# Rows as sixteen quarter-array products, index products in bf16, and a new table of places, in a fused attention and expert kernel

## The chip, the cores and the metric

The kernel runs on one core of one Trainium2 chip. The metric is the device time of one execution in microseconds (us); the kernel before has a median of 632.37 us over three runs (632.0 to 633.66).

## The reference, cut to what matters

Attention over 8 batches, 8 heads, 576 positions and 64 values per head, causal with a window of 128 and a linear bias per head; its output is the input of a layer of 8 experts, of which each token takes the one with the highest gate.

```python
scores = scale * np.matmul(q, k.transpose(0, 1, 3, 2))
scores = np.where((rel >= 0) & (rel < 128), scores + bias[None], -1e9)
attn = exp(scores - max); attn = attn / (sum + 1e-09)
x = np.matmul(attn, v).transpose(0, 2, 1, 3).reshape(B * S, H * D)     # 4608 x 512
logits = x @ w_gate                                                    # 8 experts
expert_idx = np.argmax(logits, axis=1); gate_w = softmax(logits)[expert_idx]
out[token] = gate_w[token] * (relu(x[token] @ w1[e]) @ w2[e])          # e = expert_idx[token]
```

## The kernel before

**Attention** goes over 36 chunks of 128 queries. Each chunk passes through named steps, each a few instructions on one engine:

- S00, S01, S10, S11 (`scores`, lines 201 and 206): TensorE puts bias and scores of two head pairs each into `s_ps`; there are two such buffers (g = 0, 1), one deep.
- N0, N1 (`peak`): VectorE folds and takes the negated maximum. E0, E1 (`exps`, line 228): ScalarE takes the exponentials, four instructions with an accumulator read each.
- T (`transposes`, line 242): sixteen products on TensorE into `t_ps`. P (`place`, line 250): ScalarE copies them to `pT`; GpSimd masks the window's ends (lines 253, 256).
- V, U, W, Z (`values`, line 283): products with v into `r_ps`, for one chunk or a pair. X (`copy_x`): a copy of `r_ps` to `xT`, on ScalarE for the chunks in `X_ACT` (line 293), on VectorE for the others (line 295).
- R (`rows`, line 304): `xT` times `iw`, which holds the gate's columns beside an identity, so that rows of x and the parts of the logits come out together, 72 columns a product; they go to `t_ps`, or to `s_ps` for the chunks in `ASIDE`. I, Y (`invert`, `scale_rows`, line 318): VectorE divides by the sums, and a DMA writes the rows to `xd` in device memory.

**Routing** follows in groups of three to six chunks (`route`, a generator that is resumed piece by piece): maxima, one-hot, ranks within an expert, and last the index products (line 650), which add into `base` which token stands in which slot of which expert. Their left side `lp` (128x128 per chunk, line 617) and right side `rr` (128x48, line 646) come from VectorE.

**The experts** come after: for each, gathers of its tokens' rows, two layers of which each is three products of rounded and rest parts (lines 828 and 1033), and a scatter of the result. The first layer of the largest expert's first 256 tokens is done within the end of attention (`EP`), and the weights are rounded by ScalarE and GpSimd throughout (lines 1145 and 1150).

What sets the order: up to step 147 every engine's instructions go out in the order in which the program is written. A chunk has four steps of time; the tables `PLACES`, `ALONE`, `FIRST`, `SECOND`, `BEFORE_ALONE`, `END`, `ROUND`, `REST`, `EP` and `PACE` give for each piece the step relative to its chunk and a rank within the step. Loads go out on SyncE at set steps, each made to wait for the last product before it. `WU` is the number of products of zeros (line 157) at the start and in steps 0 to 3.

```python
for k, (at, rank) in places(ch).items():
    plan.setdefault(4 * ch + at, []).append((rank, ch, k))
```

Of the kernel before, what the change touches and what calls it, by code (L numbers as in the profile page):

```python
# [425 lines left out]
ALONE = {'V': (14, 0.9), 'U': (15, 3), 'X': (16, 0.5)}
FIRST = {'X': (19, 5.5)}
SECOND = {'V': (11, 2.5), 'U': (11, 3), 'W': (14, 0.9), 'Z': (14, 2.2), 'X': (17, 0.3)}
BEFORE_ALONE = {'V': (11, 0.7), 'U': (11, 1.5), 'W': (12, 4.5), 'Z': (12, 5.5), 'X': (17, 0.3)}
QAT = (11, 0.5)  # L430
PIECES = ((1, 20),)
# [60 lines left out]
LB = 1
LW = (0, 0, 0, 0)
WU = (6, 3, 0, 0, 0)
APART_TO = 27
# [937 lines left out]
```

## Time and profile before

| | |
|---|---|
| median of three runs | 632.37 us (632.0 to 633.66) |
| profiled execution | 635.56 us, span 633.5 us |
| granted TensorE clock, mean | 0.992 |
| TensorE busy | 609.1 us (96%) |
| VectorE, ScalarE, GpSimd busy | 371.9, 298.2, 313.8 us (59%, 47%, 50%) |
| bytes moved | 99.17 MB, mean 157 GB/s |

The span is the time from the first to the last instruction of the profiled execution; the time of an execution is some 2 us longer. PE is TensorE's products, PEld its weight loads, which overlap them; DVE is VectorE, ACT ScalarE, POOL GpSimd. A product of fp32 operands stands in the trace as two records, one of bf16 operands as one. A product's duration includes its way through the array, so that several overlap: what a piece takes of TensorE's time is read from its start to the start of the next piece.

### The profile page before, as it was taken

The page shows a single profiled execution, that of the slowest core. Times are in us where ns is not written, and L with a number is a line of the kernel's source. Part 1 is how long each engine was busy: PE and PEld are TensorE (multiplying, and loading weights), DVE is VectorE, ACT ScalarE, POOL GpSimd, SP SyncE. Part 2 cuts the span into 40 slices and gives each one's busy share as a digit, 9 for nine tenths or more (in the row PEclk, how much of TensorE's full clock was granted, in tenths as well). Part 3 has the DMA queues.
Part 4 walks back from the last instruction along what each step waited for, and adds up shares of the span by engine and source line. Part 5 has one row for each costly group of instructions (what it writes and reads, how often), then busy time and mean ns, then how long its engine had stood idle before and what let it go on. Part 6 is the DMA issues. An engine that isn't in the chain of part 4 may idle for free.

```text
span 633.5 us, 17303 instructions
## 1 busy us (share of the span) xinstructions
PE 609.1 (96%) x6833; PEld 527.1 (83%) x6833; DVE 371.9 (59%) x875; ACT 298.2 (47%) x897; POOL 313.8 (50%) x465
## 2 busy tenths in 40 slices
PE   7989998999999989999999999999999999999996
PEld 5777887887878868888988898998898998888884
DVE  5667878778767775535543754555355356347411
ACT  6988887788654225423342434334233333424311
POOL 5766976877853031265236607633660760561202
PEclk9999999999979999999999999999999999999999
DMA  8777787677453265372544325434443542544201
GB/s 283 248 223 242 228 257 221 210 255 247 132 168 98 87 198 162 111 270 75 215 124 145 110 88 180 118 112 133 143 119 95 174 140 74 187 113 150 68 1 62
DMA packets 46902, 99.17 MB, mean 157 GB/s; under 512 B 12053, under 2 KB 13077, under 8 KB 46818
## 3 DMA queue, kind: packets, MB, share of 16 engines
q1 hardware_dynamic: 38194, 76.82, 37.9%
q0 software_dynamic: 8336, 20.96, 11.3%
q8 instruction: 55, 0.90, 0.6%
q10 hardware_dynamic: 288, 0.26, 0.2%
q14 instruction: 29, 0.24, 0.1%
HBM read 77.93 MB, written 20.09 MB: 155 GB/s over the span
## 4 chain that ended last, share of the span: by engine, by line
PE 76%; issue 9%; ACT 6%; POOL 4%; DVE 3%; DMA 1%; POOLq 0%; ACTq 0%; DVEq 0%
PE y_ps L1033 26%; PE l_ps L828 26%; PE r_ps L283 5%; PE s_ps L206 4%; PE t_ps L304 4%; ACT pe L228 3%; ACT pT L250 2%; PE t_ps L242 2%; PE s_ps L201 2%; PE s_ps L828 2%; PE s_ps L650 1%; POOL out L1021 1%; DVE nmax L218 1%; POOL pT L253 1%; POOL pT L256 1%
## 5 line engine op out<-in xcount | busy, mean ns | idle before, releaser
L835 DVE SCALAR_TENSOR_TENSOR hl<-l_ps,hh 128x320 fp32r<-128x320 f32 (+4 forms) x104 | 51.8, 502 | 153.4 <-ACT hh L831 127.7
L831 ACT ACTIVATE hh<-l_ps 128x320 fp32r<-128x320 f32 (+4 forms) x104 | 46.0, 447 | 202.1 <-PE l_ps L828 158.3
L808 POOL DMA_INDIRECT xg<-xd,od_idx x112 | 115.1, 1028 | 35.1 <-issue 33.1
L228 ACT ACTIVATE pe<-s_ps,nmax 128x128 f32<-128x128 f32 x288 | 102.1, 379 | 19.9 <-DVE nmax L218 11.8
L1033 PE MATMUL y_ps<-wh,hh 128*128 128x512 f32 x280 | 110.0, 393 | 0.1
L1033 PE MATMUL y_ps<-wl,hh 128*128 128x512 f32 x280 | 109.3, 390 | 0.0
L1033 PE MATMUL y_ps<-wh,hl 128*128 128x512 f32 x280 | 109.1, 390 | 0.0
L1021 POOL DMA_INDIRECT out<-y,od_pidx x33 | 34.4, 1043 | 144.8 <-ACT y L1039 138.6
L1133 DVE TENSOR_TENSOR wl<-w_raw,wh 128x512 fp32r<-128x512 f32 x114 | 73.9, 689 | 27.7 <-ACT wh L1129 21.0
L828 PE MATMUL l_ps<-xh,wh 128*128 128x320 f32 (+8 forms) x416 | 81.2, 317 | 0.2 <-ACT xh L787 0.2
L828 PE MATMUL l_ps<-xl,wh 128*128 128x320 f32 (+8 forms) x416 | 80.7, 315 | 0.7 <-issue 0.7
L828 PE MATMUL l_ps<-xh,wl 128*128 128x320 f32 (+8 forms) x416 | 80.4, 315 | 0.7 <-issue 0.7
L828 PEld LDWEIGHTS l_ps<-xh,wh 128*128 128x128 f32 x416 | 67.7, 188 | 7.4 <-issue 1.2
L828 PEld LDWEIGHTS l_ps<-xl,wh 128*128 128x128 f32 x416 | 65.9, 188 | 3.6 <-issue 1.6
L828 PEld LDWEIGHTS l_ps<-xh,wl 128*128 128x128 f32 x416 | 65.8, 188 | 2.2 <-issue 0.3
L228 ACT ACTIVATION_READ_ACCUMULATOR pe<-s_ps,nmax 128x1 f32 x288 | 62.6, 217 | 0.0
L1033 PEld LDWEIGHTS y_ps<-wh,hl 128*128 128x128 f32 x280 | 52.6, 188 | 11.4
L1033 PEld LDWEIGHTS y_ps<-wh,hh 128*128 128x128 f32 x280 | 52.6, 188 | 10.2 <-issue 0.6
L1129 ACT CAST wh<-w_raw 128x1024 fp32r<-128x1024 f32 x57 | 59.5, 1044 | 1.6 <-DMA w_raw<-w 1.4
L1033 PEld LDWEIGHTS y_ps<-wl,hh 128*128 128x128 f32 x280 | 52.6, 188 | 9.2
L206 PE MATMUL s_ps<-k_sb,q_sb 64*64 64x192 f32 (+2 forms) x1152 | 59.0, 314 | 0.0
L253 POOL TENSOR_SCALAR_AFFINE_SELECT pT<-pT 64x512 f32<-64x512 f32 x56 | 37.5, 670 | 34.6 <-ACT pT L250 32.5
(237 smaller groups left out, 905.9 us busy)
## 6 DMA issues: line engine op xcount, KB each, us to landing
w_raw<-w SPq DMA_DIRECT2D x56, 512.0 KB
v_sb<-v SPq DMA_DIRECT2D x36, 256.0 KB
xd<-x_sb SPq DMA_DIRECT2D x32, 288.0 KB
q_sb<-qT SPq DMA_DIRECT2D x35, 256.0 KB
k_sb<-kT SPq DMA_DIRECT2D x23, 256.0 KB
w_raw<-w SPq DMA_DIRECT2D x16, 256.0 KB
w_n<-w SPq DMA_DIRECT2D x4, 1024.0 KB
k_sb<-kT SPq DMA_DIRECT2D x8, 384.0 KB
```

The lines of the kernel that those rows point to most:

```text
L206: anchor(nc.tensor.matmul(out=heads[half(a), c, n, 64 * u0:].rearrange("q (u x) -> q u x", x=64), lhsT=blocks["q", ch][half(c), 2 * g + n, ...
L228: nc.scalar.activation(out=pes[ch][:, 2 * g + n, :, c, :], in_=s_ps[g][:, c, 192 * n + 64:192 * n + 192].rearrange("q (u x) -> q u x", x=6 ...
L253: nc.gpsimd.affine_select(out=to[half(c), :, 0], in_=to[half(c), :, 2], pattern=[[0, 8], [-1, 64]], base=-1, channel_multiplier=1, compare ...
L283: anchor(nc.tensor.matmul(out=tops[half(p % 2), c, p // 2, i:i + n, :], lhsT=blocks["v", j][half(c), r, p, :], rhs=diagonal(pTs[group], ha ...
L808: ins = tc.nc.gpsimd.indirect_dma_start(out=g[:, s], out_offset=None, in_=parts, in_offset=bass.IndirectOffsetOnAxis(ap=idx[:, s], axis=0),)
L828: nc.tensor.matmul(out=ps, lhsT=a[:, 128 * d:128 * d + 128], rhs=b[:, d], start=(k == 0), stop=(k == 11))
L831: nc.scalar.activation(out=hh, in_=ps, func=AF.Relu)
L835: nc.vector.scalar_tensor_tensor(out=hl, in0=ps, scalar=0.0, in1=hh.bitcast(F32), op0=ALU.max, op1=ALU.subtract)
L1021: ins = nc.gpsimd.indirect_dma_start(**kw).ins
L1033: nc.tensor.matmul(out=ys[t], lhsT=a[:, tl], rhs=b[:, 512:1024], start=(f == 0 and k == 0), stop=(f == 7 and k == 2))
L1129: keep(tc, nc.scalar.copy(out=wh, in_=raw))
L1133: keep(tc, eng.tensor_tensor(out=wl[:, sl], in0=raw[:, sl], in1=wh.bitcast(F32)[:, sl], op=ALU.subtract))
```

## The change

- `rows`: each 64x128 product is split into two of 64x64, one per half of the queries; 16 products a chunk in place of 8. With two halves of the contraction and two of the output, four tiles of the array are used in turn.
- Routing: `lp` is bf16 with two buffers in place of fp32 with one; the token's number is split into two bf16 parts (`tokh`, `tokl`), so `rr` has two parts and there are two bf16 products per chunk in place of one in fp32. The constant `tok` goes.
- `X_ACT` names 17 chunks in place of 6.
- `WU` goes from (6, 3, 0, 0, 0) to (7, 4, 1, 2, 2).
- The tables of attention's places are new, most of them by a step or a rank; `ROUND`, `REST` and the entries of chunks 0 and 1 stay. `END`, which overrides the general places for single chunks, has entries for 30 chunks in place of 11. Two or three entries of `EP` and `PACE` move by a step.
- A pad of 160 bytes (`EPAD`) in one pool.

```diff
     def rows(ch):
         for p in range(0, NP, 2):
             for c in range(2):
-                for e in range(2):
-                    anchor(nc.tensor.matmul(out=row_bank(ch)[:, e, HW * (p + c):HW * (p + c) + HW],
-                                            lhsT=xT[half(e), c, p // 2].rearrange("d a q -> d (a q)"),
-                                            rhs=iw_sb[half(e), p // 2, c, :], start=True, stop=True))
+                for a in range(2):
+                    for e in range(2):
+                        anchor(nc.tensor.matmul(out=row_bank(ch)[half(a), e, HW * (p + c):HW * (p + c) + HW], lhsT=xT[half(e), c, p // 2, a, :],
+                                                rhs=iw_sb[half(e), p // 2, c, :], start=True, stop=True))
...
-PLACES = {'S10': (-1, 9), 'S11': (0, 2), 'E0': (0, 2.5), 'T': (5, 0.7), 'N1': (1, 0.7), 'P': (5, 0.95), 'S00': (-3, 4.7), 'S01': (-3, 6), 'R': (22, 1), 'E1': (2, 2), 'N0': (-2, 1.5), 'I': (21, 0.5), 'Y': (23, 1.8)}
+PLACES = {'S10': (-1, 9), 'S11': (0, 2), 'E0': (0, 0.95), 'T': (5, 0.7), 'N1': (1, 1.8), 'P': (5, 6.5), 'S00': (-3, 3.7), 'S01': (-3, 6.5), 'R': (22, 1), 'E1': (2, 2), 'N0': (-2, 2.5), 'I': (21, 9), 'Y': (23, 2.5)}
...
-X_ACT = (20, 21, 25, 32, 33, 34)
+X_ACT = (3, 7, 9, 10, 11, 12, 13, 14, 15, 16, 20, 21, 25, 26, 32, 33, 34)
...
-LB = 1
-WU = (6, 3, 0, 0, 0)
+WU = (7, 4, 1, 2, 2)
...
-    lp = rp.tile(sp3, F32, name="lp", bufs=LB)
+    lp = rp.tile(sp3, BF16, name="lp")
...
-    rr = rp.tile(sc3, F32, name="rr")
-    nc.vector.tensor_tensor(out=rr, in0=eq, in1=st["tok"][:, c0:c0 + G].unsqueeze(2).to_broadcast(sc3), op=ALU.mult)
+    rr = rp.tile([128, G, 2, E * TT], BF16, name="rr")
+    for k, n in enumerate(("tokh", "tokl")):
+        nc.vector.tensor_tensor(out=rr[:, :, k, :], in0=eq,
+                                in1=st[n][:, c0:c0 + G].unsqueeze(2).to_broadcast(sc3), op=ALU.mult)
     yield
     ip = spare(st, 1, E * TT)
     for g in range(G):
-        nc.tensor.matmul(out=ip, lhsT=lp[:, g, :], rhs=rr[:, g, :], start=g == 0, stop=g == G - 1)
+        for k in range(2):
+            nc.tensor.matmul(out=ip, lhsT=lp[:, g, :], rhs=rr[:, g, k, :], start=(g == k == 0),
+                             stop=(g == G - 1 and k == 1))
```

Three places in the order of instructions, each from before and from the change.

TensorE, the first group's index products and the next rows, before (`lp`, `rr` are the sides of the index products, `pT` and `v_sb` those of the values):

```order
L206 MATMUL s_ps<-k_sb,q_sb 64x192 x8
L650 MATMUL s_ps<-rr,lp 128x48 x5
L283 MATMUL r_ps<-pT,v_sb 64x64 x24
L304 MATMUL t_ps<-iw_sb,xT 128x72 x8
L283 MATMUL r_ps<-pT,v_sb 64x64 x24
```

The same place in the change; its five pairs of index products have a weight load ahead of each, and eight rows of bias products stand before line 206:

```order
L242 MATMUL t_ps<-c_sb,pe 128x64 x16
L652 LDWEIGHTS lp
L652 MATMUL s_ps<-rr,lp 128x48
...
L206 MATMUL s_ps<-k_sb,q_sb 64x192 x8
L283 MATMUL r_ps<-pT,v_sb 64x64 x24
L305 MATMUL t_ps<-iw_sb,xT 64x72 x16
L283 MATMUL r_ps<-pT,v_sb 64x64 x24
```

The index products move ahead of a half of the scores; the rows stay between the two halves of the values.

ScalarE, from the exponentials before chunk 12's pT copy to chunk 13's and on, before (`x8` are the eight exponentials of two half chunks):

```order
L228 ACTIVATE pe,rsum<-s_ps,nmax 128x2x64 x8
L250 COPY pT<-t_ps 128x8x128
L228 ACTIVATE pe,rsum<-s_ps,nmax 128x2x64 x8
L250 COPY pT<-t_ps 128x8x128
L228 ACTIVATE pe,rsum<-s_ps,nmax 128x2x64 x4
L1145 CAST wh<-w_raw 128x512
```

and in the change:

```order
L228 ACTIVATE pe,rsum<-s_ps,nmax 128x2x64 x8
L250 COPY pT<-t_ps 128x8x128
L228 ACTIVATE pe,rsum<-s_ps,nmax 128x2x64 x8
L293 COPY xT<-r_ps 128x512 x2
L250 COPY pT<-t_ps 128x8x128
L228 ACTIVATE pe,rsum<-s_ps,nmax 128x2x64 x4
L1149 CAST wh<-w_raw 128x512
```

Two copies of X, of a pair of chunks, now stand ahead of a pT copy.

TensorE at the start, the second half of chunk 1's scores and chunk 0's transposes, before:

```order
L201 LDWEIGHTS eye_sb
L201 MATMUL s_ps<-bias_sb,eye_sb 64x384
L206 MATMUL s_ps<-k_sb,q_sb 64x192 x8
L242 MATMUL t_ps<-c_sb,pe 128x64 x16
L201 LDWEIGHTS eye_sb
```

and in the change, where the pair of line 157 stands twice (`x_sb` holds zeros there):

```order
L201 LDWEIGHTS eye_sb
L201 MATMUL s_ps<-bias_sb,eye_sb 64x384
L206 MATMUL s_ps<-k_sb,q_sb 64x192 x4
L157 LDWEIGHTS x_sb
L157 MATMUL t_ps<-x_sb 128x512
...
L206 MATMUL s_ps<-k_sb,q_sb 64x192 x4
L242 MATMUL t_ps<-c_sb,pe 128x64 x16
```

Two products of zeros stand inside the scores, ahead of the transposes.

## Rows read from the trace of the kernel before

**Rows 1.** The page, part 1: busy time, share of the span, instructions.

```profile
PE 609.1 (96%) x6833; PEld 527.1 (83%) x6833; DVE 371.9 (59%) x875; ACT 298.2 (47%) x897; POOL 313.8 (50%) x465
```

**Rows 2.** Busy time by stretch; the last three columns are clock, DMA share, GB/s.

```profile
0.00:27.00 27.00, 21.80 (x441) 16.20 (x441) 16.48 (x36) 20.46 (x91) 17.32 (x45) 1.00 0.82 268
27.00:165.00 138.00, 130.55 (x3230) 109.80 (x3228) 107.91 (x228) 112.95 (x483) 104.05 (x192) 1.00 0.74 232
165.00:214.00 49.00, 47.09 (x855) 40.17 (x852) 34.46 (x112) 23.11 (x83) 21.58 (x41) 0.93 0.37 113
```

**Rows 3.** Timeline of TensorE: start, duration, line, shape, records; the rows of one chunk.

```profile
93.73 1.11 PE L304 MATMUL t_ps<-iw_sb,xT 64*128 64x72 f32 x16
94.77 0.67 PE L283 MATMUL r_ps<-pT,v_sb 64*64 64x128 f32 x16
```

**Rows 4.** Groups by shape on TensorE: one from 27 to 165 us, three to 214.

```profile
L304 PE MATMUL t_ps<-iw_sb,xT 64*128 64x72 f32 x400 | 27.9, 279 | 1.8 <-ACT pT L250 1.7
...
L304 PE MATMUL t_ps<-iw_sb,xT 64*128 64x72 f32 x96 | 7.7, 308 | 1.3 <-ACT pT L250 1.3
L650 PE MATMUL s_ps<-rr,lp 128*128 128x48 f32 x30 | 3.8, 275 | 0.0
L304 PE MATMUL s_ps<-iw_sb,xT 64*128 64x72 f32 x48 | 3.3, 277 | 0.2 <-DVE e_gate L789 0.2
```

**Rows 5.** Timeline of TensorE: index products of a group of six, and what follows.

```profile
166.23 1.54 PE L650 MATMUL s_ps<-rr,lp 128*128 128x48 f32 x12
167.70 1.12 PE L304 MATMUL t_ps<-iw_sb,xT 64*128 64x72 f32 x16
```

**Rows 6.** Timeline of TensorE: value products of 128 and of 64 columns.

```profile
168.74 2.22 PE L283 MATMUL r_ps<-pT,v_sb 64*64 64x128 f32 x80
170.78 0.34 PE L201 MATMUL s_ps<-bias_sb,eye_sb 64*64 64x384 bf16 x4
...
183.83 1.63 PE L283 MATMUL r_ps<-pT,v_sb 64*64 64x64 f32 x96
185.28 0.34 PE L201 MATMUL s_ps<-bias_sb,eye_sb 64*64 64x384 bf16 x4
```

**Rows 7.** Timeline of TensorE after attention: small products in bf16.

```profile
225.07 0.34 PE L800 MATMUL l_ps<-od_two,sel 128*128 128x42 bf16 x7
225.26 0.48 PE L1033 MATMUL y_ps<-wh,e_hh 128*128 128x512 f32 x1
```

**Rows 8.** Groups by shape, 27 to 165 us: count, busy us, mean ns, idle before.

```profile
L293 ACT COPY xT<-r_ps 128x512 f32<-128x512 f32 x3 | 1.8, 610 | 1.0 <-PE r_ps L283 1.0
L295 DVE COPY xT<-r_ps 128x512 f32<-128x512 f32 x23 | 15.0, 683 | 0.7 <-ACT xT L293 0.6
L646 DVE TENSOR_TENSOR rr<-eq,c_sb 128x240 f32<-128x240 f32 x3 | 1.2, 399 | 0.0
```

**Rows 9.** Timeline of TensorE and ScalarE at the start; idle before in brackets.

```profile
6.04 0.82 PE L157 MATMUL t_ps<-x_sb 128*128 128x512 bf16 x3
7.57 0.36 PE L201 MATMUL s_ps<-bias_sb,eye_sb 64*64 64x384 bf16 x4 [0.71 <-ACT pe L228]
8.97 0.36 PE L201 MATMUL s_ps<-bias_sb,eye_sb 64*64 64x384 bf16 x4 [0.39 <-ACT pe L228]
...
10.07 0.37 ACT L228 ACTIVATE pe<-s_ps,nmax 128x128 f32<-128x128 f32 x1 [1.15 <-PE s_ps L206]
```

**Rows 10.** Stretch of the low clock (columns as rows 2), and TensorE there.

```profile
176.40:183.20 6.80, 6.80 (x80) 4.98 (x80) 5.96 (x12) 4.42 (x21) 3.70 (x10) 0.50 0.73 226
...
176.16 1.75 PE L304 MATMUL t_ps<-iw_sb,xT 64*128 64x72 f32 x16 [1.28 <-ACT pT L250]
177.84 0.54 PE L201 MATMUL s_ps<-bias_sb,eye_sb 64*64 64x384 bf16 x4
```

**Rows 11.** Waits, 27 to 165 us: who for whom, us, times, longest.

```profile
ACT pe L228 <- DVE nmax L218: 8.5, 8, 2.0
...
ACT pT L250 <- PE t_ps L242: 7.0, 12, 1.0
```

More of the change, by code (lines that the diff above doesn't have):

```diff
@@ L422, in attention @@
         step(s)
-PLACES = {'S10': (-1, 9), 'S11': (0, 2), 'E0': (0, 2.5), 'T': (5, 0.7), 'N1': (1, 0.7), 'P': (5, 0.95), 'S00': (-3, 4.7), 'S01': (-3, 6), 'R': (22, 1), 'E1': (2, 2), 'N0': (-2, 1.5), 'I': (21, 0.5), 'Y': (23, 1.8)}
[L426 to L429, printed above, removed]
@@ L430 @@
-QAT = (11, 0.5)
-PIECES = ((1, 20),)
+PLACES = {'S10': (-1, 9), 'S11': (0, 2), 'E0': (0, 0.95), 'T': (5, 0.7), 'N1': (1, 1.8), 'P': (5, 6.5), 'S00': (-3, 3.7), 'S01': (-3, 6.5), 'R': (22, 1), 'E1': (2, 2), 'N0': (-2, 2.5), 'I': (21, 9), 'Y': (23, 2.5)}
+ALONE = {'V': (14, 0.5), 'U': (14, 6.5), 'X': (16, 2.2)}
+FIRST = {'X': (21, 1.8)}
+SECOND = {'V': (10, 1.8), 'U': (11, 6.5), 'W': (14, 0.5), 'Z': (14, 2.2), 'X': (16, 1.8)}
+BEFORE_ALONE = {'V': (10, 0.5), 'U': (12, 4.3), 'W': (12, 4.5), 'Z': (13, 1.5), 'X': (16, 1.8)}
@@ L432 @@
+QAT = (11, 2.2)
+PIECES = ((1, 2.2),)
 ROUND = [(23, 1.8), (32, 1.8), (41, 1.8), (50, 1.8), (59, 1.8), (68, 1.8), (77, 1.8), (86, 1.8), (95, 1.8), (104, 1.8), (113, 1.8), (122, 1.8), (131, 1.8), (140, 1.8)]
 REST = [(24, 0.5), (33, 0.5), (42, 0.5), (51, 0.5), (60, 0.5), (69, 0.5), (78, 0.5), (87, 0.5), (96, 0.5), (105, 0.5), (114, 0.5), (123, 0.5), (132, 0.5), (141, 0.5)]
-X_ACT = (20, 21, 25, 32, 33, 34)
+X_ACT = (3, 7, 9, 10, 11, 12, 13, 14, 15, 16, 20, 21, 25, 26, 32, 33, 34)
 ASIDE = (31, 33, 35)
-END = {0: {'V': (7, 1), 'U': (7, 3), 'X': (8, 0.5), 'R': (10, 1), 'I': (10, 4), 'Y': (11, 2)}, 1: {'V': (10, 0.9), 'U': (11, 3), 'X': (12, 0.5), 'R': (14, 1), 'I': (14, 4), 'Y': (15, 2)}, 30: {'R': (22, 2.5), 'I': (21, 2.5), 'Y': (22, 3.2), 'W': (11, 3.3), 'Z': (13, 0.5)}, 31: {'R': (19, 3), 'I': (18, 3.7), 'Y': (19, 3.2), 'V': (15, 1.8), 'N1': (0, 4.7)}, 32: {'X': (15, 1), 'R': (16, 3), 'I': (13, 0.95), 'Y': (16, 3.2), 'E1': (2, 2.5), 'P': (5, 1.8), 'S10': (-1, 0.95)}, 33: {'V': (9, 3.5), 'U': (9, 3.6), 'W': (9, 6.5), 'Z': (10, 3.1), 'X': (11, 1.1), 'R': (13, 1), 'I': (13, 1.1), 'Y': (13, 1.2)}, 34: {'V': (8, 1), 'U': (8, 1.1), 'X': (8, 2), 'R': (9, 3), 'I': (9, 3.1), 'Y': (9, 9), 'S10': (-1, 3.3)}, 35: {'T': (2, 9), 'P': (3, 2.5), 'V': (5, 2.2), 'U': (6, 1.1), 'X': (6, 2.2), 'R': (6, 3), 'I': (6, 3.1), 'Y': (6, 3.2)}, 27: {'E0': (-1, 6.5)}, 7: {'S11': (0, 6.5)}, 6: {'S10': (-1, 8)}}
@@ L491 @@
 RB = 2
-LB = 1
 LW = (0, 0, 0, 0)
-WU = (6, 3, 0, 0, 0)
+WU = (7, 4, 1, 2, 2)
 APART_TO = 27
-PACE = {21: (128, 129, 131, 133, 135, 137, 139), 27: (140, 141, 142, 145, 146), 30: (145, 146)}
-EP = {0: ((30, 'z'),), 52: ((30, 'o'),), 146: ((2.5, '2'), (3.53, '3')), 142: ((8, 'p0'), (8, 'p1')), 145: ((5.5, '1'),), 130: ((3.3, 'g'),), 143: ((4.7, '0'),)}
+PACE = {21: (128, 129, 131, 133, 135, 137, 139), 27: (140, 141, 142, 144, 145), 30: (145, 146)}
+EP = {0: ((30, 'z'),), 52: ((30, 'o'),), 146: ((2.5, '2'), (6.5, '3')), 142: ((8, 'p0'), (8, 'p1')), 130: ((3.3, 'g'),), 145: ((0.3, '0'), (8, '1'))}
 LE = ('45', '', '6')
@@ L507 @@
 COLS = {p: 512 for p, c in enumerate(CAPS) if 496 <= c < 512}
-APAD, PPAD, MPAD = 256, 320, 160
+EPAD, APAD, PPAD, MPAD = 160, 256, 320, 160
 LINE = 32
@@ L769, in slot_sum @@
     nc.vector.tensor_tensor(out=acc if idx is None else idx, in0=ps[:, 1:2], in1=acc, op=ALU.add)
-CONSTS = (("ident", 128), ("seq", MAXOV), ("rev", E), ("prof", E), ("tokh", N // 128), ("tokl", N // 128), ("tok", N // 128), ("i128", 128), ("grp", 1))
+CONSTS = (("ident", 128), ("seq", MAXOV), ("rev", E), ("prof", E), ("tokh", N // 128), ("tokl", N // 128), ("i128", 128), ("grp", 1))
 def gather_rows(tc, st, g, idx, n=N + 1, **kw):
@@ L854, in step @@
             x["idx"] = pool.tile([128, 2], U32, name="e_idx")
+            space(pool, EPAD)
             for n in "hl":
@@ L1404, in consts @@
     iw = np.concatenate([np.stack([np.stack([head(p, c) for c in range(2)], axis=1) for p in (e, e + 2)], axis=1) for e in range(2)])
-    parts = dict(ident=np.eye(128), seq=np.broadcast_to(np.arange(MAXOV), (128, MAXOV)), prof=np.broadcast_to(CAPS, (128, E)), rev=np.broadcast_to(np.arange(E, 0, -1), (128, E)), tokh=-64 * (back // 64), tokl=-(back % 64), tok=-back,
+    parts = dict(ident=np.eye(128), seq=np.broadcast_to(np.arange(MAXOV), (128, MAXOV)), prof=np.broadcast_to(CAPS, (128, E)), rev=np.broadcast_to(np.arange(E, 0, -1), (128, E)), tokh=-64 * (back // 64), tokl=-(back % 64),
                  i128=np.broadcast_to(np.arange(128), (128, 128)), grp=np.arange(128)[:, None] // 32)
```

1 line of the change is left out of this document (added).

## The prediction

> **What bounds the kernel now.** I read the page's busy shares first: TensorE (PE) is busy 96% of the span, no other engine over 59% [rows 1]. That is an average over two unlike stages, so I cut the span by time [rows 2]: start to 27 us, the middle of attention to 165 us, its end to 214 us, and the expert layers after it. The change touches attention and routing alone, so the 419 us from 214 to the end stay as they are. In the middle PE is busy 130.55 of 138.0 us (94.6%), ScalarE (ACT) 112.95 (81.8%), VectorE 107.91, GpSimd 104.05. So PE has a lead of 17.6 us over the next engine, and no more: what PE gains beyond that, another engine takes. The end, 47.09 of 49.0 us, is PE alone; ACT is at half there.
>
> What PE spends on the parts that change is the distance from one start to the next. Rows of one chunk stand in 16 records (each fp32 product is two) and take 1.04 us, 93.73 to 94.77 [rows 3]. The index products of a group of six take 1.47 us, 166.23 to 167.70, for 12 records: 0.122 us each [rows 5].
>
> **Rows.** A 64x128 product becomes two of 64x64: 32 records a chunk, each on a quarter of the array. The nearest row is the value products, which already run in quarters: 96 records of 64 columns take 183.83 to 185.28, so 15.1 ns each [rows 6]; at 128 columns 80 records take 168.74 to 170.78, 25.5 ns [rows 6]. Rows have 72 columns; a line between the two gives 16.4 ns, so 0.53 us a chunk, between 0.48 and 0.82. I take 0.53, since 72 lies next to 64: 0.51 us less per chunk. Of 36 chunks, 25 have their rows in the middle (400 records of 16 each), 9 at the end (96 and 48) [rows 4], 2 before: 12.8 us off PE in the middle, 4.6 at the end, 1 in the start.
>
> The rule of the Trainium skill that speaks against this stands in "TensorE: Matmul & The Clock Gate", section "Wait — 56ns, not 53.3ns?": matmul starts never come closer than about 25 ns, however few the columns. By it 32 records would take 0.80 us; the 15.1 ns of [rows 6] disagree, and I go by the row.
>
> **Index products.** 35 fp32 products become 70 in bf16. The nearest row is another set of small bf16 products, seven of 42 columns from 225.07 to 225.26, 27 ns each [rows 7]. A group of five falls from 10 x 0.122 = 1.22 us to 0.27, one of six from 1.47 to 0.32, one of three by 0.4. At the other end a bf16 record costs what an fp32 one does and nothing is won. Three groups of five lie in the middle: 2.85 us. Two of six and one of three lie at the end (30 records [rows 4]): 2.7 us. One more comes after 214, where the chain soon waits for a gather; I count it nothing, and at most 0.95. The price is VectorE's: the second part of the right side is one more multiply per group, 0.40 us [rows 8], so some 1.7 us in the middle, under 30 us of idle. The left side keeps its size and input, and gets a second buffer.
>
> **X copies.** Eleven more copies of attention's output go to ACT, all in the middle, at 0.610 us [rows 8]: 6.7 us more for ACT; VectorE loses 11 x 0.683 = 7.5 [rows 8]. The order shows them ahead of a pT copy, two in a row for a pair of chunks; the pT copy, the exponentials behind it, GpSimd's masks and the value products wait for them there.
>
> **Zero products.** Seven more stand in the start: one at first, one before chunk 1's scores, three between their halves and two inside the second half. PE idles 0.71 us before the first of these halves and 0.39 before the second [rows 9]; three such products took 0.82. The six after the first meet 1.6 us of work with 1.1 us of holes. The exponentials at 10.07 had waited 1.15 us for that second half [rows 9], so what doesn't fit is paid: I take 0.7 us, between 0 and 1.6. The granted clock there is 1.00, so none is to be won back.
>
> **Places.** The sequence on PE keeps its pattern (scores, transposes, scores, values around rows); what moves is by one or two pieces. I price it at nothing by itself, but it sets how well engines that are nearly equal interlock. The clock comes in here too: at 176.4 us it fell to 0.50 for 6.8 us [rows 10], with 1.28 us of PE idle before. There a chunk's rows took 1.68 us, 176.16 to 177.84, against 1.04 at 1.00 [rows 3, 10]; at that ratio 6.8 us hold 4.2 us of work, and one such stretch costs 2.6. I leave it as it is: a freed PE could shift it away, and could open another.
>
> **The sum.** Middle: PE falls to 130.55 - 12.8 - 2.85 = 114.9, ACT rises to 112.95 + 6.7 = 119.65, VectorE goes to 102.1, GpSimd stays at 104. The bound passes from PE to ACT. If the stage packs its busiest engine as it packs PE now, at 94.6%, it takes 126.5 us: 11.5 less, not the 15.65 that PE loses. End: PE loses 4.6 + 2.7 = 7.3, and since nearly all of its chain is PE, I take 7. Start: 0.7 more. In all 17.8 us less. The profiled execution took 635.56 (span 633.5), the median of the runs is 632.37, 3.2 lower; the difference carries over, and 632.37 - 17.8 gives 614.6. With the ends of the unknown terms and one low-clock stretch more or less, this case spans 608 to 621.
>
> **The rivals.** *PE stays the bound.* If ACT packs closer than 94.6%, its holes closed by the new places, the middle is 114.9/0.946 = 121.5 (16.5 less), the low-clock stretch goes (7 + 2.6 less at the end) and the start costs nothing: 26.1 less, 606. For it: before, ACT had 25 us of idle in the middle. Against: no engine but PE has yet been over 82%.
>
> *A floor per product.* If a small record costs what one of 128 columns does, 25.5 ns, rows take 0.82 and save 0.22. The middle has PE at 122.2, so 129.2 us (8.8 less), the end 4.7 less, the start 0.7 more: 12.8 less, 619.6. Against it stands the 15.1 ns. The page named above would have it so.
>
> *The sixteen don't overlap four deep.* Then rows cost what they do now and the change doesn't do what it says; the index products alone leave the middle 2.9 shorter, the end 2.7, the start 0.7 longer: 627.5. The value products, of the same shape, speak against it.
>
> *Slower: ACT's queue.* Copies wait in line before the work of the next chunk. Today ACT's three copies of X in the middle idled 1.0 us before them [rows 8], a third of a microsecond each; the other work on ACT waits 8.5 us for VectorE's maxima and 7.0 for PE's transposes [rows 11]. If ACT stays at the 81.8% it has reached so far, 119.65 us of work takes 146.2, and eleven more waits of 0.33 make it 149.9: 11.9 more in the middle, 7 less at the end, 0.7 more in the start, 638.0. It decides at an ACT share of 119.65/144.3 = 82.9% in the middle: above, time is won in all. For it: four engines would stand at 102 to 120 us, with loops through all of them. The Trainium skill, "TensorEngine Tiling (Array Packing)", section "PSUM Bottleneck", says that tiling quickens TensorE but not the copies out of PSUM, which may then be the bottleneck; no run here shows that yet, and by it the gain in the middle would be small. Against: the waits of 8.5 and 7.0 end with PE's scores and transposes, which come earlier now.
>
> **How the numbers follow.** The forecast gets 0.60, PE as the bound 0.14, the floor 0.10, no overlap 0.04, ACT's queue 0.12. About 0.3% (2 us) is what a measurement of this kernel can tell from no change. The first four are all faster by more: 0.88. The last spreads around 638, with 0.03 within 2 us and 0.09 over. The range reaches down to PE as the bound with a little beyond, 605, and up past the floor and two low-clock stretches more, 625; outside lie no overlap, ACT's queue and a piece of the lowest case.
>
> **What would show it.** Right: rows of a chunk at 0.5 to 0.6 us from start to start, and of the same shape as the value products; index products of a group near 0.3 us; the stage that was 138 us near 126, with ACT the busiest engine at 90% or more and PE near 115; attention over about 18 us earlier, and the stage after it of the same length. Wrong: rows at 0.8 or 1.0 (the floor, no overlap); PE idle in the middle, ended by ACT's pT copies or exponentials, with ACT under 83%; more stretches at a granted clock of 0.50; or a stage after attention that grows by what attention lost, because a gather or the routing of the last chunk, not PE, ends it.

## The result, and the profile after

The changed kernel takes 627.25 us (median, 626.7 to 627.93), the one before 633.01 in the same comparison: a ratio of 0.9909 [0.9887, 0.9932], 5.8 us less where 17.8 were forecast, and outside the range of 605 to 625. The profiled execution took 626.93 us, with a span of 624.9.

What the change does to TensorE is on the page, part 1 of the kernel after; before it was 609.1 us [rows 1]:

```profile
PE 586.2 (94%) x7416; PEld 507.1 (81%) x7416; DVE 366.9 (59%) x871; ACT 303.1 (49%) x908; POOL 316.8 (51%) x465
```

By stretch, to be held against [rows 2] (columns: stretch, its length, busy us and instructions of PE, PE's weight loads, VectorE, ScalarE, GpSimd; clock, DMA share, GB/s):

```profile
27.00:165.00 138.00, 118.80 (x3652) 100.44 (x3652) 102.94 (x224) 117.49 (x496) 104.83 (x195) 1.00 0.76 234
165.00:214.00 49.00, 42.73 (x1022) 36.09 (x1019) 39.60 (x139) 24.34 (x87) 21.42 (x39) 1.00 0.42 129
```

In the 138 us of the middle PE works 118.80 us in place of 130.55, and nobody took the place: ScalarE has 117.49. So the stage should be shorter. It hardly is. Stages can be dated by events that exist in both kernels; the transposes of a chunk (L242) are such. On TensorE's timeline of the kernel after, chunks 4, 31 and 35, and the first product of the experts' second layer:

```profile
27.12 0.71 PE L242 MATMUL t_ps<-c_sb,pe 64*128 64x64 f32 x16
...
164.19 0.71 PE L242 MATMUL t_ps<-c_sb,pe 64*128 64x64 f32 x16
...
189.46 0.71 PE L242 MATMUL t_ps<-c_sb,pe 64*128 64x64 f32 x16 [0.19 <-DVE x_sb L318]
...
203.77 0.48 PE L1037 MATMUL y_ps<-wh,e_hh 128*128 128x512 f32 x1
```

The same four of the kernel before:

```profile
27.07 0.71 PE L242 MATMUL t_ps<-c_sb,pe 64*128 64x64 f32 x16
...
164.65 0.71 PE L242 MATMUL t_ps<-c_sb,pe 64*128 64x64 f32 x16
...
193.16 0.71 PE L242 MATMUL t_ps<-c_sb,pe 64*128 64x64 f32 x16
...
209.26 0.48 PE L1033 MATMUL y_ps<-wh,e_hh 128*128 128x512 f32 x1
```

From here on "the middle" is the time from chunk 4's transposes to chunk 31's, "the end" from there to that first product. The middle went from 137.6 to 137.1 us, the end from 44.6 to 39.6. Nearly all that the change gives in attention comes out in the end. The middle of the kernel before, and of the one after (columns as above):

```profile
27.07:164.65 137.58, 130.13 (x3218) 109.45 (x3217) 107.51 (x227) 112.73 (x482) 103.63 (x192) 1.00 0.74 233
```

```profile
27.12:164.19 137.07, 117.87 (x3631) 99.70 (x3629) 102.04 (x221) 117.36 (x493) 103.97 (x194) 1.00 0.76 235
```

The parts on TensorE are as forecast. A chunk's rows, then the value products behind them; and the index products of a group of six, to be held against [rows 3, 5]:

```profile
107.09 0.68 PE L305 MATMUL t_ps<-iw_sb,xT 64*64 64x72 f32 x32
107.59 0.83 PE L283 MATMUL r_ps<-pT,v_sb 64*64 64x192 f32 x16
...
182.75 0.46 PE L652 MATMUL s_ps<-rr,lp 128*128 128x48 bf16 x12 [0.27 <-DVE nmax L218]
```

Rows take 0.50 us here from start to start in place of 1.04; the median of the middle's 25 places is 0.55. Twelve index records end 0.46 us after the first starts, and follow on one another at 25 to 28 ns in the seven groups.

So TensorE waits instead. Its idle time (neither a product nor a weight load running) in the middle rose from 7.2 us in 20 holes to 18.8 in 37. Part of it is waiting for other engines, as the view of waits shows for 27 to 165 us (who for whom, us in all, times, longest); before, the first row stood at 6.8 us and the second at 4.2:

```profile
DVE s_ps L216 <- PE s_ps L206: 21.4, 21, 2.8
...
PEld L201 <- issue: 11.8, 21, 2.0
ACT pT L250 <- POOL wl L1154: 6.9, 2, 3.5
PE s_ps L201 <- ACT pe L228: 5.9, 11, 1.8
...
PEld s_ps L206 <- issue: 4.8, 6, 1.7
...
PE s_ps L206 <- issue: 4.1, 6, 1.3
```

VectorE waits three times as long for scores as before (21.4 us): it stands idle for PE while PE stands idle for it and for ScalarE. I read that as a ring without slack, not one full engine; the experiments test it. The rows with "issue" are the second part: the engine waited for nothing that the trace records. (A row of PEld counts the loads' own idle time, much of it under running products, so this part is taken from PE's holes.) Of the 18.8 us, 6.7 in 11 holes are of this kind, and before there were none. Ahead of nine of them the next instruction names no semaphore; ahead of two, 0.70 us at 52.98 and 0.87 at 104.87, it names one whose last update lay earlier. (The 5.8 us of some expectations leave the second of these out.) Two of the holes on TensorE's timeline after:

```profile
41.66 0.48 PE L206 MATMUL s_ps<-k_sb,q_sb 64*64 64x192 f32 x2
43.48 0.88 PE L206 MATMUL s_ps<-k_sb,q_sb 64*64 64x192 f32 x14 [1.34 <-issue]
...
75.99 0.84 PE L206 MATMUL s_ps<-k_sb,q_sb 64*64 64x192 f32 x15
77.94 0.32 PE L206 MATMUL s_ps<-k_sb,q_sb 64*64 64x192 f32 x1 [1.11 <-issue]
```

PE stops in the middle of one line's products, whose first two had already begun, and goes on 1.1 to 1.3 us later. What stands around such holes is the loading of TensorE's own instructions: a queue on the page (part 3) moves them in 16 KB pieces. The view of DMA queues for 41.1 to 42.1 us shows one piece (columns: packets, MB, share of 16 engines; 5.8% of 16 x 1.0 us is 0.93 us):

```profile
q8 instruction: 1, 0.02, 5.8%
```

The piece landed at 42.05, the hole began at 42.15 and ended at 43.48, 1.43 us after the landing. All the others follow suit. TensorE's instructions in the trace (products, weight loads and its sequencer's own) can be numbered in the order of their starts, from 0: there are 14915, and 59 pieces of 256 would hold 15104. Each of the eleven holes ends at an instruction whose number is 193 above a multiple of 256 (1729, 1985, 2241, 2753, 3265, 3521, 3777, 4545, 5057, 5825, 6081), and 1.23 to 1.59 us after a piece landed. The middle has 28 such borders; at the other 17 there is no such hole. The kernel before has 26 of them in its middle; the instruction there starts 1.57 us or more after a piece's landing, 3.1 in the median, and no hole of this kind is found. So these holes are TensorE's instructions arriving late.

### The profile page after: what moved, and what is told of

The parts are those of the page before. It is cut to its first block, busy times and chain, and to the rows that moved or that the text cites. A ratio compares the mean times of both kernels' runs of the same rounds, so it can differ in the third digit from the quotient of the medians.

```text
span 624.9 us, 18463 instructions
## 1 busy us (share of the span) xinstructions
PE 586.2 (94%) x7416; PEld 507.1 (81%) x7416; DVE 366.9 (59%) x871; ACT 303.1 (49%) x908; POOL 316.8 (51%) x465
## 4 chain that ended last, share of the span: by engine, by line
PE 63%; POOL 12%; issue 11%; ACT 7%; DVE 4%; DMA 2%; POOLq 0%; SPq 0%; DVEq 0%; ACTq 0%
PE l_ps L831 25%; PE y_ps L1037 24%; ACT pe L228 3%; ACT pT L250 3%; PE r_ps L283 3%; PE s_ps L206 3%; POOL xg L811 2%; POOL pT L256 2%; POOL pT L253 2%; PE s_ps L831 2%; PE t_ps L242 1%; POOL out L1025 1%; PE s_ps L201 1%; DMA xg<-xd,idx 1%; PE t_ps L305 1%
## 5 line engine op out<-in xcount | busy, mean ns | idle before, releaser
L811 POOL DMA_INDIRECT xg<-xd,od_idx x112 | 117.5, 1049 | 35.0 <-issue 31.9
L206 PE MATMUL s_ps<-k_sb,q_sb 64*64 64x192 f32 (+2 forms) x1152 | 60.9, 307 | 4.1 <-issue 4.1
L228 ACT ACTIVATION_READ_ACCUMULATOR pe<-s_ps,nmax 128x1 f32 x288 | 63.9, 222 | 0.0
L283 PE MATMUL r_ps<-pT,v_sb 64*64 64x64 f32 (+2 forms) x1728 | 55.0, 260 | 3.0 <-issue 1.5
```

Of the source, the lines that this page charges most:

```text
L206: anchor(nc.tensor.matmul(out=heads[half(a), c, n, 64 * u0:].rearrange("q (u x) -> q u x", x=64), lhsT=blocks["q", ch][half(c), 2 * g + n, ...
L228: nc.scalar.activation(out=pes[ch][:, 2 * g + n, :, c, :], in_=s_ps[g][:, c, 192 * n + 64:192 * n + 192].rearrange("q (u x) -> q u x", x=6 ...
L283: anchor(nc.tensor.matmul(out=tops[half(p % 2), c, p // 2, i:i + n, :], lhsT=blocks["v", j][half(c), r, p, :], rhs=diagonal(pTs[group], ha ...
L811: ins = tc.nc.gpsimd.indirect_dma_start(out=g[:, s], out_offset=None, in_=parts, in_offset=bass.IndirectOffsetOnAxis(ap=idx[:, s], axis=0),)
```

## The experiments

First the numbers on which the verdicts rest, each from one profile. Idle is PE's in the middle; "late" is that part of it which ended at a border of instruction pieces, 1.0 to 1.7 us after a piece had landed. ScalarE and PE are busy us in the middle. A dash: whole time not compared. Stretches at the lower clock (granted 0.50), each 3.4 or 6.8 us long as a whole, lie in the middle of a_oldx (6.8 us), a_wl (3.4), a_rmoved (1.5) and a_rmoved2 (11.9 in all), and in the end of before (6.8), after again, b_rows, b_split, a_oldx and a_wl (3.4 each); the lengths stand as measured, and a 6.8 us stretch costs some 2.6 us by the estimate of the prediction.

| kernel | ratio to before | middle | PE | PE idle (late) | ScalarE | end |
|---|---|---|---|---|---|---|
| before | 1 | 137.6 | 130.1 | 7.2 (0.0) | 112.7 | 44.6 |
| before, again | - | 137.4 | 130.3 | 6.9 (0.0) | 112.9 | 43.6 |
| after | 0.9909 | 137.1 | 117.9 | 18.8 (6.7) | 117.4 | 39.6 |
| after, again | - | 137.5 | 117.3 | 19.9 (6.8) | 117.6 | 39.1 |
| b_rows | 0.9952 | 135.0 | 120.8 | 13.9 (5.1) | 112.4 | 45.3 |
| b_idx | 0.9966 | 136.4 | 127.9 | 8.2 (0.3) | 112.7 | 42.4 |
| b_rows_idx | 0.9905 | 134.7 | 118.6 | 15.7 (4.8) | 112.3 | 42.7 |
| a_oldrows | 0.9977 | 139.3 | 128.9 | 10.1 (0.0) | 118.3 | 41.5 |
| a_oldplaces | 0.9979 | 136.1 | 117.2 | 18.4 (4.9) | 116.9 | 42.8 |
| a_oldx | 0.9910 | 140.5 | 119.1 | 20.9 (4.7) | 113.0 | 39.2 |
| b_split | 1.0106 | 144.9 | 138.3 | 6.3 (1.5) | 113.5 | 43.9 |
| a_bf16rows | - | 130.3 | 109.8 | 19.9 (1.5) | 117.4 | - |
| a_noaccum | - | 132.1 | 116.2 | 15.6 (6.4) | 99.3 | - |
| a_bf16_noaccum | - | 123.8 | 107.4 | 16.1 (1.5) | 99.6 | - |
| b_noaccum | - | 135.2 | 129.9 | 5.3 (0.3) | 93.7 | - |
| a_noq | - | 134.8 | 117.1 | 17.3 (4.1) | 117.4 | - |
| a_wl | 0.9973 | 139.6 | 117.7 | 21.4 (2.9) | 118.1 | 39.9 |
| a_halfsum | 0.9934 | 137.0 | 117.0 | 19.7 (6.9) | 108.3 | 40.7 |
| a_rmoved | - | 156.5 | 117.5 | 38.5 (0.8) | 118.6 | - |
| a_rmoved2 | - | 164.0 | 121.9 | 41.6 (1.1) | 118.3 | - |

**Second profiles.** Both kernels unedited once more.

> The changed kernel once more, unedited, for a second profile. If the middle (transposes of chunk 4 to those of chunk 31, 137.1 us in the first profile) is the kernel's own: 136 to 138 us and 5 to 7 us of TensorE's idle time without a semaphore. If it is one execution's: anything from 134 to 141 us, as the kernels with the same rows have shown. In neither case the forecast's 126 us.

> The kernel before once more, unedited, for a second profile. TensorE bounds its middle, and little waits: 137 to 138.5 us, under 1 us of idle time without a semaphore. If one execution differs from another as much as the kernels with sixteen-product rows do: 135 to 140 us.

Middles of 137.5 us after and 137.4 before, against 137.1 and 137.6: "not shorter" is the kernels' own, not one execution's. So are the holes: ten of them again end at the same number above a multiple of 256 (192; one record is missing from this trace). The end goes from 43.6 to 39.1 us, 4.4 less; between the two profiles without a low clock there (before again, and after) it is 4.0. Three things turned out to be one execution's: the low clock at 176.4 us [rows 10] is absent from the second profile of before (clock 1.00 there, and an end 1.0 us shorter); the second profile of after has 3.4 us of it at 176.0, the first none; and what lies behind the end, 3.1 us shorter in the first pair of profiles, is 0.3 shorter in the second.

**The parts alone: rows, index, both.** The change's sixteen products, its index products, or both, put into the kernel before, with the old tables:

```
-                for e in range(2):
-                    ... out=row_bank(ch)[:, e, ...], lhsT=xT[half(e), c, p // 2] (128 columns)
+                for a in range(2):
+                    for e in range(2):
+                        ... out=row_bank(ch)[half(a), e, ...], lhsT=xT[half(e), c, p // 2, a, :]
```

> The kernel before with sixteen 64x64 row products alone (old places, old index products). Three theories for the 12 us of TensorE work that the middle of attention lost without getting shorter. Loop (GpSimd's masks and ScalarE's copies form a ring that was as long as TensorE's work): the middle to the 32nd transposes keeps its length, the end saves about 4, so some 629. Code (twice the row instructions must be loaded, TensorE waits for them without a semaphore): TensorE idle with no semaphore of 3 us or more in the middle, some 627 to 630. Places (the new places eat the gain): the rows alone save 10 to 16, so 617 to 623.

> The kernel before with the index products in two bf16 parts alone; nothing is left out. By the forecast's own price it takes 0.95 us a group off TensorE in six groups of five chunks and 1.15 in two of six, some 5 us of work in the middle and 1 to 2 us in the end. If TensorE bounds before: 627 to 630 us where before has 633 (ratio 0.990 to 0.995). If the middle is held by the ring already: only the end's group shows, 0.996 to 1.000.

> The kernel before with both kinds of new products, old places, old X copies, old zero products. Loop: 626 to 628, the index products adding about 2 at the end to the rows' 4. Code: 625 to 628 (index products add 35 instructions in all, no more stalls than with rows alone). Places: 612 to 618.

Rows alone: 0.9952 [0.9922, 0.9982]; index alone: 0.9966 [0.9944, 0.9988]; both: 0.9905 [0.9873, 0.9938], the product of the two within their intervals, and the same as the whole change. The middle's windows, b_idx first:

```profile
27.20:163.50 136.30, 127.86 (x3218) 107.21 (x3216) 108.81 (x231) 112.67 (x482) 103.55 (x190) 1.00 0.74 234
```

```profile
27.10:161.80 134.70, 118.65 (x3618) 99.22 (x3616) 107.67 (x231) 112.27 (x480) 102.77 (x190) 1.00 0.76 237
```

The index products take 2.3 us off PE and shorten the middle by 1.2. Both parts together take 11.5 off PE and shorten it by 2.9. The late instructions come with the rows, 5.1 us of holes with rows alone and 4.8 with both, and not with the index products, 0.3. With rows alone the middle is 135.0, so it did not keep its length as the theory of the loop had it, nor did the time fall by the 10 to 16 us of the theory of places.

**The rows undone in the changed kernel.**

```
-                for a in range(2):
-                    for e in range(2):
+                for e in range(2):
```

> The changed kernel with eight 64x128 row products a chunk again (0.5 us more TensorE work each, half the row instructions). Loop: the middle hardly changes, the end grows by 4, 630 to 632. Code: stalls without a semaphore vanish and give back what the rows cost, 627 to 630. Places: no statement of its own; with a bound TensorE 640.

0.9977 [0.996, 0.9995], middle 139.3 us. PE works 11.0 us more than after, but the middle is only 2.3 longer, and not one late instruction is left. Of the 11.0 us that the sixteen products free, PE stands 6.7 in such holes.

**The other parts undone: places, X copies.**

```
-PLACES = {... 'E0': (0, 0.95), ... 'N1': (1, 1.8), 'P': (5, 6.5), ...}
+PLACES = {... 'E0': (0, 2.5), ... 'N1': (1, 0.7), 'P': (5, 0.95), ...}
```

(and the other tables of places, as before) and

```
-X_ACT = (3, 7, 9, 10, 11, 12, 13, 14, 15, 16, 20, 21, 25, 26, 32, 33, 34)
+X_ACT = (20, 21, 25, 32, 33, 34)
```

> The changed kernel with the tables of places of before (its X copies and zero products stay). Loop: within 2 us of the changed kernel, 625 to 630. Code: the same, since the instructions are the same. Places: 612 to 620.

> The changed kernel with the six X copies on ScalarE of before (eleven go back to VectorE). If ScalarE's queue takes part in the loop: 2 to 5 faster than the changed kernel, 622 to 625. If the loop is GpSimd's or the code's: within 2 of the changed kernel.

Old places with the new X copies: 0.9979 [0.9944, 1.0014]. Old X copies with the new places: 0.991 [0.9884, 0.9936], as the whole. Since b_rows_idx, with old places and old X copies, has 0.9905 too, the tables win nothing of themselves; they make up for what the copies' move, or the zero products that both of these kernels keep, costs under the old tables, and shift time between stages: middle 134.7 to 137.1, end 42.7 to 39.6 from b_rows_idx to after. The middle of a_oldx, 140.5, holds 6.8 us at the lower clock and says nothing of the copies; its whole time does.

**More, but wider, instructions.** If the count of TensorE's instructions were what its loading cannot follow, 32 more records a chunk in the kernel before should stall it. Each score product cut in two:

```
-  rhs=batch[b][half(c), i - 2 + u0:i + 1, 2 * g + n, :]
+  for lo, hi in ((u0, 2), (2, 3)) if u0 < 2 else ((2, 3),):
+      rhs=batch[b][half(c), i - 2 + lo:i - 2 + hi, 2 * g + n, :]
```

> The kernel before with each score product of two or three key blocks cut in two at the last block: 16 more products, so 32 more records with their loads, a chunk, twice what the rows' change adds, with the same columns in sum and nothing changed on the other engines. Code: TensorE, without a semaphore to wait for, stands idle 6 us or more in the middle (none of it in the kernel before, some 5 with sixteen rows), and the time grows by 6 to 14, 638 to 648. Loop: instruction counts don't matter; TensorE's scores lengthen by a few hundredths of a microsecond, 633 to 636.

1.0106 [1.008, 1.0131], yet it is PE's work that costs (130.1 to 138.3 us), not late instructions: 1.5 us, again at borders of 256. Both expectations fell: the 6 us of stalls, and the few hundredths of a microsecond a chunk. The count alone fell as an explanation. What remains is the pace: value products, rows and value products in a row are 128 records at mostly 15 to 17 ns, and with their 128 weight loads they use up 256 instructions, a whole piece, in some 2 us. The pieces of the middle took 0.9 to 2.4 us each to move.

**The rows out of that run of short records.** In the changed kernel, rows of chunks 2 to 29 go between the two halves of a chunk's scores, or (second kernel) behind both:

```
-'R': (22, 1), ... 'Y': (23, 2.5)
+'R': (23, 9.5), ... 'Y': (24, 0.5)      second: 'R': (24, 2.1), 'Y': (24, 3.0)
```

> The changed kernel with the sixteen row products of chunks 2 to 29 moved on TensorE from between two groups of value products to between the two halves of a chunk's scores of heads 2 and 3 (and their scaling on VectorE after it); nothing is left out and TensorE's work is the same. Theory of code loading (TensorE runs out of its own instructions where values, rows and values follow on one another, 128 records at 15 to 17 ns): the bursts are 48 records at most of each kind with scores between them, the idle time without a semaphore in 27-165 us falls from about 6 us to under 3, and the middle from 137.1 to 133-136 us unless the later maximum gives it back. Rival, the stalls come with the number of records, not their place: still 4.5 to 6.5 us without a semaphore. Time: 0.995 to 1.003 of the changed kernel's 627.3 us; 0.55 us per chunk later for the maximum of heads 2 and 3 can cost up to 28 x 0.55 = 15 us if that ring is tight, which would show as a middle of 140 us or more.

> The changed kernel with the row products of chunks 2 to 29 moved behind all of a chunk's scores, ahead of the next transposes, which use the same tile and so wait for the rows' scaling on VectorE; nothing is left out. Theory of code loading: values no longer touch rows, the idle time without a semaphore in 27-165 us falls under 3 us. But transposes now wait for rows, then scaling: up to 1 us per chunk of new waiting behind VectorE's semaphore, where TensorE has nothing else in order to do: middle 134 to 150 us. Time 627 to 640 us. Rival (stalls by number of records): 4.5 to 6.5 us without a semaphore remain and the new wait comes on top.

What lies behind attention differs in both, so only attention is read. Holes of late instructions fall to 0.8 and 1.1 us with the same 3630 products, as the theory of code loading said. But the middle grows to 156.5 and 164.0 us, far past the 140 us that the first expectation named and the 150 of the second. Waits of the first, 27 to 165 us:

```profile
PEld t_ps L242 <- DVE x_sb L318: 19.3, 20, 1.0
...
PE s_ps L201 <- ACT pe L228: 13.5, 18, 1.8
PE t_ps L242 <- DVE x_sb L318: 12.8, 20, 0.7
```

Transposes now wait for the scaling of rows, which had been over in time, and 0.55 us of later scores come back as 0.7 us per chunk. The longer middle also loads fewer instructions per us, so this pair by itself supports the code theory without settling it; the borders of 256 do. In the middles of all twenty profiles 100 holes stand ahead of an instruction that names no semaphore, and every one is at such a border.

**Bf16 rows, no sums, both.** These cut PE's records (16 in place of 32), ScalarE's accumulator reads, or both, and are read in attention only.

```
-xTs[ch] = xp.tile([128, 2, 2, 2, 64], F32, ...)
+xTs[ch] = xp.tile([128, 2, 2, 2, 64], BF16, ...)       (and iw_sb in BF16)
```

```
-func=AF.Exp, bias=..., scale=1.0, accum_out=sums[ch // 2][...])
+func=AF.Exp, bias=..., scale=1.0)                      (sums set to 64)
```

> The changed kernel with rows and their right side in bf16: 16 records a chunk in place of 32, as many as before the change, and still less TensorE work; the rows lose precision, so experts' counts can pass their sizes, and only attention is to be read. Code: idle of TensorE without a semaphore in the middle falls from 5.8 us to under 1.5, and the 32nd transposes come 4 to 6 us earlier, near 159. Loop: TensorE's work is not what bounds, so the 32nd transposes come within 2 us of 164.

> Left out: the sums of the exponentials (the 288 accumulator reads on ScalarE, 222 ns each in the changed kernel's profile, 8 a chunk); the sums are set to a constant, so the rows' scale, the gates and everything behind attention differ, and only attention is read: the time from the transposes of chunk 4 to those of chunk 31, 137.1 us in the changed kernel (137.6 before). Theory A, the ring of scores, maximum and exponentials with ScalarE as its busiest engine holds the middle: ScalarE loses up to 216 x 0.22 = 48 us of 117 there, TensorE becomes the bound at about 118 us of work, and the stretch falls to 123-131 us. Theory B, TensorE's stalls without a semaphore (about 6 us) and its own work hold it, ScalarE does not: the stretch stays at 134-138 us. Rival C, VectorE (maximum and folding on one tile per pair of heads) holds the ring: also 134-138 us, but with TensorE's idle time then behind VectorE's semaphore instead of ScalarE's.

> The changed kernel with rows from bf16 (16 records a chunk in place of 32) and without the sums of the exponentials: only attention is read. Alone, bf16 rows gave 130.3 us from the transposes of chunk 4 to those of chunk 31 and no sums 132.1, against 137.1. Theory A, two costs that stand in series (stalls for instructions, and ScalarE's part of the ring): about 137.1 - 6.8 - 5.0 = 125 us. Theory B, one chain that either of them relaxes, something third (VectorE's maxima, GpSimd's masks, scores on one tile) next in line: 129 to 131 us.

> The kernel before with the sums of the exponentials left out (accumulator reads on ScalarE, 219 ns each, 8 a chunk; sums set to a constant, so only attention is read). In the changed kernel the same cut shortened the stretch from the transposes of chunk 4 to those of chunk 31 from 137.1 to 132.1 us. Theory A: before, TensorE's 130.5 us of work bounds that stretch (137.6 us), and ScalarE's relief buys little: 135 to 138 us. Theory B, the ring over ScalarE bound already before the change and TensorE never did: 130 to 134 us.

The windows of a_bf16rows, a_noaccum, a_bf16_noaccum and b_noaccum over their middles:

```profile
27.70:158.00 130.30, 109.79 (x3230) 92.10 (x3228) 102.00 (x221) 117.40 (x493) 104.08 (x194) 1.00 0.79 247
```

```profile
26.10:158.20 132.10, 116.18 (x3630) 98.82 (x3628) 101.50 (x222) 99.31 (x275) 104.01 (x206) 1.00 0.77 245
```

```profile
26.30:150.10 123.80, 107.37 (x3230) 90.01 (x3228) 100.82 (x221) 99.59 (x275) 104.05 (x206) 1.00 0.83 262
```

```profile
25.80:161.00 135.20, 129.86 (x3216) 108.20 (x3216) 106.79 (x227) 93.73 (x262) 103.24 (x203) 1.00 0.75 237
```

Less from PE (8.1 us of work, 5.2 of late instructions) gives 6.7; 18 us less from ScalarE give 5.0; both give 13.3, a little over the sum. (The reads took 222 ns each, but the next exponential starts before a read ends, so 216 of them took 18 us off ScalarE and not the 48 of the expectation.) So PE and ScalarE act as costs in series on one path, and neither engine is "the bound". Nor are the DMA engines: their share is 0.76 in the middle of after and 0.83 in the shortest. The expectation that ScalarE's relief would make PE the bound at its 118 us fell: 132.1 against 123 to 131, with 15.6 us of PE idle. Before the change the same relief gives 2.4 us, with PE busy 129.9 of 135.2: there PE was nearly all of the path.

**GpSimd, VectorE, and half of the sums.** Without GpSimd's scaling of q (scores unscaled, attention only); with the second weight parts on VectorE; with half of the sums formed by VectorE:

```
-todo += [(QAT[1], n, lambda ch=ch: scale_q(nc.gpsimd, ch)) ...]
```

```
-nc.gpsimd.tensor_tensor(out=wl[:, sl], ...)
+nc.vector.tensor_tensor(out=wl[:, sl], ...)
```

```
+nc.vector.tensor_reduce(out=sums[...][:, ch % 2, n, 0, :], in_=pes[ch][:, n]...)   (no accum_out for g = 0)
```

> The changed kernel without GpSimd's scaling of the queries by 1/8 (left out from the second chunk on), so 20 us less GpSimd work in the middle; the scores change and with them the experts' counts, so only attention is to be read. Loop through GpSimd: the masks of pT come earlier and the 32nd transposes come 5 to 10 us earlier, 154 to 159. Code: GpSimd doesn't matter, the 32nd transposes come within 2 us of 164 and the idle without a semaphore stays near 5.8.

> The changed kernel with the second part of each weight piece of the attention stage (wl) formed on VectorE instead of GpSimd; nothing is left out. GpSimd loses the pieces that stand ahead of the masks of the turned exponentials, VectorE (102.9 us of 138 in the middle) gains them. If GpSimd's masks behind those pieces hold the chain (10.5 + 6.7 + 3.7% of the middle's chain are GpSimd's): middle 133 to 136 us and 0.992 to 0.998 of the changed kernel. If the ring over VectorE holds it: VectorE's pieces of 0.7 us stand ahead of maxima and the middle gets longer, 138 to 142 us, 1.000 to 1.008.

> The changed kernel with the sums of the first pair of heads' exponentials formed by VectorE from the exponentials (two reductions of 128x256 a chunk) instead of ScalarE's accumulator reads; nothing is left out. ScalarE loses 4 x 0.226 = 0.9 us a chunk, VectorE gains about 2 x 0.3 to 0.4 = 0.6 to 0.8 us a chunk (the 128x512 reduction for the maximum takes 0.69). Theory A, ScalarE is the tightest in the middle (117.5 us against VectorE's 102.9): middle 134 to 136 us, 0.993 to 0.998 of the changed kernel. Theory B, the ring holds by its latency over both: VectorE's reductions stand ahead of maxima and the middle gets no shorter, 137 to 141 us, 1.000 to 1.006.

Taking 14.6 us off GpSimd (104.0 to 89.3) gives 2.2 us, where 5 to 10 were expected if the loop ran through it. Moving 10.3 us from GpSimd to VectorE: 0.9973 [0.995, 0.9997], worse than the change as it is (its middle of 139.6 holds 3.4 us at the lower clock). Taking 9.0 us from ScalarE and giving VectorE 15.3: middle 137.0, 0.9934 [0.9917, 0.995], no better. Its window:

```profile
27.50:164.50 137.00, 117.02 (x3632) 98.83 (x3630) 117.37 (x276) 108.34 (x383) 104.04 (x194) 1.00 0.77 236
```

Work moved between these engines gained nothing. No run beat the change by more than the intervals; b_rows_idx equals it with far fewer edits.

## Why the prediction was wrong

**Rows: right.** 32 records in 0.55 us a chunk in the median against 0.53, 16.4 ns each in the median and 18.0 on the mean; the floor of about 25 ns in the Trainium skill ("TensorE: Matmul & The Clock Gate", section "Wait — 56ns, not 53.3ns?") does not hold for four 64x64 products on separate quarters, as [rows 6] had said. That rival and "no overlap" fell with it.

**Index products: right.** 25 to 28 ns a record against 122; the groups (columns as in [rows 4, 8]), with VectorE's second multiply at 0.58 us where 0.40 was taken:

```profile
L305 PE MATMUL t_ps<-iw_sb,xT 64*64 64x72 f32 x800 | 19.3, 226 | 2.6 <-ACT pT L250 2.4 <-issue 0.2
...
L293 ACT COPY xT<-r_ps 128x512 f32<-128x512 f32 x14 | 8.1, 622 | 0.1
L646 DVE TENSOR_TENSOR rr<-eq,c_sb 128x240 bf16<-128x240 f32 x6 | 3.2, 580 | 0.0
L652 PE MATMUL s_ps<-rr,lp 128*128 128x48 bf16 x30 | 1.3, 184 | 0.0
```

**PE's work in the middle: nearly right.** 12.3 us less, where 15.65 were summed. Of the missing 3.4, 1.3 is in the rows (18.0 ns on the mean of 800 records, not 16.4) and 0.6 in the index products (2.3 alone, not 2.85). The rest lies, I think, at the new holes, where a record's end stands alone instead of under the next one; that was not tried.

**X copies: right in price, without effect.** 14 copies at 0.622 us, 0.610 before. ScalarE's work in the middle rose by 4.6 us, not 6.7; undoing the move changes no time.

**Zero products: in the range, below the 0.7 us.** Chunk 4's transposes start at 27.12 against 27.07 in the first pair of profiles and at 27.55 against 27.04 in the second: 0.05 to 0.5 us.

**The low clock: one execution's.** It was left out of the sum, rightly, and comes and goes between profiles of one kernel.

**The end: work right, length not.** PE 42.70 us before, 39.97 in the profile without the low clock, 33.32 after: 6.7 less, where 7.3 were worked out. The end is 4.0 to 5.0 us shorter, not 7: PE's idle time there rises to 6.0 us, from 1.9 in the first profile of before and 3.4 in the second. "Nearly all of its chain is PE" held before; with that much less of PE it no longer does.

**The sum of the middle: the step that failed.** "If the stage packs its busiest engine as it packs PE now, at 94.6%, it takes 126.5 us" carried a packing from one engine to another. 94.6% is what PE reached when PE alone was long and each of the others had some 25 us of slack or more. With PE at 117.9, ScalarE at 117.4, GpSimd at 104.0 and VectorE at 102.0 us, ScalarE reached 117.4 of 137.1, 85.6%, so that the middle lost 0.5 us and not 11.5. By the waits above, the loop from scores through maximum and exponentials back to the scores' tile has no slack then, and each engine waits for the others in turn; that neither PE nor ScalarE alone holds the middle is shown by the runs that left work out, the loop itself is read from the waits. The runs show what a microsecond is worth in this state: from PE (work and late instructions together) about half, 6.7 of 13, from ScalarE 5.0 of 18, from GpSimd 2.2 of 14.6. And of the 12.3 us that PE freed it stood 6.7 (6.8 in the second profile) waiting for late instructions, of which no view of the kernel before held any; that term was missing altogether.

**The slower rival had the mechanism, at the wrong strength.** It kept ScalarE at 81.8% and set the turning point of the whole time at 82.9%; ScalarE came to 85.6%, above it, so time was won in all, but in the middle hardly any. Its cause, copies that wait in ScalarE's queue, is not borne out: with eleven of them back on VectorE the time is the same. The Trainium skill, "TensorEngine Tiling (Array Packing)", section "PSUM Bottleneck", says that tiling speeds TensorE but not the copies out of PSUM. This trace agrees so far that a copy still takes 0.622 us and that 12.3 us less of PE gave 0.5; that these copies are what then holds the middle, no run here shows. "PE stays the bound" at 606 fell.

What could not be settled: how many microseconds of the middle the late instructions cost by themselves, since the run that took most of them away (a_bf16rows, 6.7 to 1.5 us) took 8.1 us of work off PE too; and what VectorE's share in the loop is, since no run took work off VectorE alone.

## What to carry to other kernels

A packing share belongs to an engine with slack around it: once four engines stand within 15% of one another, price a saving at a half or less of its size, or find out by leaving work out (not moving it) on one engine at a time and on two together. Splitting products to use more of the array makes more and shorter instructions; look for waits that end in "issue" in the runs of the shortest records, and number the instructions there: holes at a fixed distance from multiples of 256 are late instructions. Here they took back more than half of the time that the array won. And before tuning an order anew, time the bare arithmetic change with the old order: here it was the whole gain.

## What the runs showed of the hardware that was not expected

TensorE can stop for up to 1.9 us with nothing to wait for that the trace shows, even in the middle of one line's products, because its own instructions arrive late. It did so 11 and 10 times in the two middles of the kernel after, 6 to 11 times in the others where fp32 rows of sixteen products stand between values, and not at all or once, for 0.3 us, with rows of eight fp32 products and whole scores. The stops lie at every 256th instruction alone, and end 1.0 to 1.7 us after a 16 KB piece has landed. The instruction queue over the whole kernel after (page, part 3: packets, MB, share of 16 engines) moves 59 pieces, one every 4.8 us on the mean of the middle, each taking 0.9 to 2.4 us:

```profile
q8 instruction: 59, 0.97, 0.7%
```

And a product of 64x64 with 72 columns in fp32, run on the four quarters of the array in turn, follows the one before at 16.4 ns in the median (14 to 33); the same number of columns on two halves took 65 ns [rows 3].
